# Clustered attention kernel: the spread of the softmax sums and the move of q's low part take other places in the order of issue

## The chip, the cores and the metric

One core of one Trainium2 chip runs the whole kernel in one launch. The metric is device time in microseconds (us), lower is better. Three runs of the kernel before gave 749.48 us as the median (748.42 to 750.17).

## The reference

Attention with a cluster mask feeds two gated mixtures of matrix products. Only the attention is touched by the change:

```python
q_n, k_n, c_n = (x / (norm(x) + 1e-6) for x in (q, k, centroids))
q_assign = argmax(q_n @ c_n.T)          # 16 clusters
k_assign = argmax(k_n @ c_n.T)
scores = where(q_assign == k_assign, q @ k.T / 8, -1e9)
attn = exp(scores - max(scores)); attn = attn / (sum(attn) + 1e-9)
x = attn @ v                            # (2, 8, 768, 64), float32
x = ((x @ w1) * (x @ w2) @ w3) @ w_out  # first mixture
out = (sigmoid(x @ w_gate) * (x @ w_val)) @ w_out2
```

## The kernel before, in words

The kernel has two stages, and the second (the matrix products of the mixtures, from 227 us on) is untouched. The first stage is the attention. It takes the 16 heads as 8 **pairs** `pr` = 0 to 7 of two heads `e` = 0, 1. Each head has 768 queries, taken in three blocks of 256, so that a pair is 6 **blocks**, `at` = 0 to 5. A block is written here as (pair, block): (3, 5) is the sixth block of pair 3. One pass of the loop `for i in range(-2, NB + 2)` writes the instructions of one block for all engines. The order on each engine is the order in which the code is written; nothing reorders it. An instruction that waits therefore holds up all that stands behind it on its engine.

What a block does, by engine:

- **TensorE** (PE): scores of two tiles of 128 queries (`s`, L340), transposes of the exponentials (`pt`, L373), and the products with v (`av`, L415 and L416). Values are carried as a high and a low part, so that a product is made of several.
- **VectorE** (DVE): the row maximum of each score tile (`nm`, L352), the low part of most transposed tiles (`pl`, L403), and pieces of the mask for the next pair. Among these are the comparison with the row's best cluster (`sm`, L268, in `prep_argmax`, block 1) and the one-hot code (`oh`, L279, block 2).
- **ScalarE** (ACT): the exponentials (`e`, L363), the high part of the transposed tiles (`ph`, L391), or a plain copy of them (`pc`, L388) where GpSimd is to split them.
- **GpSimd** (POOL): splits the first transposed tile of blocks 0, 1, 2 and 4 into high (`ph`, L54) and low part (`pl`, L59). It also finishes the pair before: `add_x` (`xa<-xa,xb`, L470, block 3), `norm_x` (`xa<-xa,r`, L474, block 5) and `split_x` (`x`, L54 and L59, right behind).
- **SyncE** (SP) issues every DMA, in the written order. Moves between partitions (`move`, L62) are DMAs too.

How a pair's softmax sums travel: at the end of a pair `turn_sums` and `store_sums` put the reciprocals into DRAM (`r_dram<-rt`, L458). Three blocks into the next pair `spread` (L465) reads them back, each row broadcast to 64 partitions, into the tile `r`. `norm_x` on GpSimd waits for `r`. The tiles `r` and `xb` share one buffer, so `spread` also waits for `add_x`, which reads `xb` last.

How operands are made: for the pair after the next (`later`) the code splits q and k into high and low (`split_lo_q` is the VectorE instruction `lo`, L218). Then `prep_scatter` moves the 64 partitions of a head to their places in the operand tiles `QH`, `KH`, `QX`, `KX`. `prep_mask` moves the one-hot codes of a head behind them (four small moves per head, the tile `ohT`).

Of the kernel before, what the change touches and what calls it, by code (L numbers as in the profile page):

```python
# [27 lines left out]
def tile_cluster_attention__then__moe__then__gated_moe(  # L28
# [32 lines left out]
    def move(dst, src):  # L61
        nc.sync.dma_start(dst.bitcast(F32), src.bitcast(F32))  # L62
# [97 lines left out]
    raw = {}  # L160
# [5 lines left out]
    def load_qk(pr):  # L166
        for w in range(2):
            t = core.tile([128, S], F32, tag="raw", name=f"raw{pr}_{w}", bufs=4)
            nc.sync.dma_start(t, qkT[pr, :, w, :])
            raw[pr, w] = t  # L170

    def load_v(pr, e=None):
        if e != 1:
            raw[pr, "v"] = core.tile([128, 2, KT, D], F32, tag="vraw", name=f"vraw{pr}", bufs=1)
        which = slice(0, 2) if e is None else slice(e, e + 1)
        nc.sync.dma_start(raw[pr, "v"][:, which], v[pr][:, which])


    opnd = {}
# [11 lines left out]
    def split_lo_q(pr):  # L191
        scaled_lo(opnd[pr, "hl"][1], raw[pr, 0], opnd[pr, "hl"][0])
# [20 lines left out]
    def operands(pr, e):  # L213
        opnd[pr, e] = tuple(core.tile([rows, S], F32R, tag=tag, name=f"{tag}{pr}_{e}", bufs=3) for tag, rows in (("QH", 96), ("KH", 96), ("QX", 128), ("KX", 128)))
        return opnd[pr, e]
# [4 lines left out]
    def prep_scatter(pr, e):  # L220
        prep_scatter_hi(pr, e)
        prep_scatter_lo(pr, e)

    def prep_scatter_hi(pr, e):
        qh, ql, kh, kl = opnd[pr, "hl"]
        r = slice(64 * e, 64 * e + 64)
        QH, KH, QX, KX = operands(pr, e)
        parts = [(QH[0:64], qh), (KH[0:64], kh), (QX[0:64], qh), (KX[64:128], kh)]
        if pr > 2:
            parts = parts[1::2] + parts[0::2]  # L230
        for to, part in parts:
            move(to, part[r])

    def prep_scatter_lo(pr, e):
        qh, ql, kh, kl = opnd[pr, "hl"]
        r = slice(64 * e, 64 * e + 64)
        QH, KH, QX, KX = opnd[pr, e]
        move(KX[0:64], kl[r])
        move(QX[64:128], ql[r])

    HALF = S // 2

    def prep_sims(pr):

        sp = ps_t.tile([128, 2, 256], F32, tag="t", name=f"sims{pr}").rearrange("p a b -> p (a b)")
        for n in range(4):
            w, half = divmod(n, 2)
            rows, cols = slice(32 * n, 32 * n + 32), slice(HALF * half, HALF * half + HALF)
            nc.tensor.matmul(sp[rows, 0:HALF], cw[:, pr % NP, :], raw[pr, w][:, cols], start=True, stop=True)
        del raw[pr, 0], raw[pr, 1]  # L250
        opnd[pr, "sims"] = sp

    def prep_sum(pr):
# [32 lines left out]
    def prep_mask(pr, e):  # L286
        ohT = opnd[pr, "oh"]
        QH, KH, _, _ = opnd[pr, e]
        halves = [slice(HALF * h, HALF * h + HALF) for h in range(2)]
        if pr == 0 and e == 0:  # L290
            for h in range(2):
                nc.vector.tensor_scalar(out=KH[64:96, halves[h]], in0=ohT[64 + 32 * h : 96 + 32 * h], scalar1=-1.0, scalar2=BIG, op0=ALU.add, op1=ALU.mult)
                nc.scalar.copy(QH[64:96, halves[h]], ohT[32 * h : 32 * h + 32])
            return
        if pr == 0:
            for h in range(2):
                nc.scalar.activation(KH[64:96, halves[h]], ohT[64 + 32 * h : 96 + 32 * h], AF.Copy, scale=BIG, bias=-BIG)
            nc.scalar.copy(QH[64:96, halves[0]], ohT[0:32])
            move(QH[64:96, halves[1]], ohT[32:64])
            return  # L300
        if e == 0:
            nc.gpsimd.tensor_scalar(out=ohT[64:128], in0=ohT[64:128], scalar1=-1.0, scalar2=BIG, op0=ALU.add, op1=ALU.mult)
        for h in range(2):
            at = 32 * h + C * e
            move(QH[64 : 64 + C, halves[h]], ohT[at : at + C])
            move(KH[64 : 64 + C, halves[h]], ohT[64 + at : 64 + at + C])
# [8 lines left out]
    NB = len(blocks)  # L315
    END = NPR - 1
# [122 lines left out]
    def invert(pr):  # L439

        ss = acc_x[pr, "sum"]
        nc.vector.reciprocal(ss, ss)
# [11 lines left out]
    def store_sums(pr):  # L454
        rp = acc_x.pop((pr, "rp"))
        rt = core.tile([2 * KT, 128], F32, tag="rt", name=f"rt{pr}", bufs=1)
        nc.vector.tensor_copy(rt, rp)
        nc.sync.dma_start(r_dram[pr], rt)  # L458

    def spread(pr, tag, bufs):  # L460

        r = core.tile([128, S], F32, tag=tag, name=f"r{pr}", bufs=bufs)
        for e in range(2):
            row = r_dram[pr, KT * e : KT * e + KT, :].rearrange("t q -> (t q)")
            nc.sync.dma_start(r[64 * e : 64 * e + 64], row.unsqueeze(0).broadcast_to([64, S]))  # L465
        acc_x[pr, "r"] = r

    def add_x(pr):
        xa = acc_x[pr, 0]
        nc.gpsimd.tensor_tensor(out=xa, in0=xa, in1=acc_x[pr, "xb"], op=ALU.add)  # L470
# [63 lines left out]
    hl = [core.tile([128, S], F32R, tag=tag, name=f"{tag}0_{w}", bufs=2) for w in range(2) for tag in ("hi", "lo")]  # L534
    opnd[0, "hl"] = hl
    QH, KH, QX, KX = operands(0, 0)
# [12 lines left out]
    nc.scalar.activation(hl[0][up], q[up], AF.Copy, scale=0.125)  # L549
    prep_split_1_hi(0)  # L550
    prep_sims(0)
    warm(28, "warm2")
    scores(0)
# [29 lines left out]
    if True:  # L583
        for i in range(-2, NB + 2):
            pr, at = divmod(i, 6)
            nxt = pr + 1 if 0 <= i and pr + 1 < NPR else None
            later = nxt + 1 if nxt and nxt + 1 < NPR else None
# [9 lines left out]
            if i == 0:  # L597
                prep_code(0, 1)
                prep_onehot(0, 1)
                prep_turn(0, 1)  # L600
                prep_sims(1)
                prep_sum(1)
            if i == NB - 1:
                store_sums(pr)
            if later and at == 0 and pr:
                load_qk(later)
            if at == 0 and 0 < pr and i < NB:
# [8 lines left out]
            if nxt and nxt > 2 and at == 1:  # L616
                prep_scatter_lo(nxt, 1)
            if nxt and at == 3:
                for e in range(2):
                    if nxt == e == 1:  # L620
                        prep_scatter(1, 1)
                    prep_mask(nxt, e)
                    if nxt == 2 and e == 0:
                        prep_scatter_lo(2, 1)
            split_lo(i - 1, 2)
# [11 lines left out]
                split_x(pr - 1)  # L637
            if nxt == 1 and at == 2:
                load_v(nxt)
            if 0 < pr and i < NB and at == 3:  # L640
                add_x(pr - 1)
                spread(pr - 1, "xb", 1)
            exponentials(2 * i + 3)
# [17 lines left out]
            if i == 1:  # L661
                prep_scatter(1, 0)
            if later and at == 5:
                prep_scatter(later, 0)
            loads = ((6, 2), (7, 1), (7, 3))
            if (pr, at) in loads:
                convert(1 + loads.index((pr, at)))
# [2 lines left out]
            if similar:  # L670
                prep_sims(similar)
# [40 lines left out]
            exponentials(2 * i + 4)  # L712
            if 0 <= i < NB - 2 and at == 4:
                invert(pr)
            if later and pr > 1 and at == 4:
                split_lo_q(later)
            if i == NB - 2:
                end_move(0)
# [37 lines left out]
    at = 0.0  # L756
# [73 lines left out]
    for n, (m, u) in enumerate(order):  # L830
# [6 lines left out]
        if n in W34_AT:  # L837
# [4 lines left out]
            for half in range(2):  # L842
                hl = wo_pool.tile([128, 2, HK, 128], F32R, tag="w3", name=f"w3_{j}_{half}", bufs=3)
# [437 lines left out]
```

## Time and profile before

| what | value |
|---|---|
| three runs, median | 749.48 us (748.42 to 750.17) |
| the profiled execution | 747.86 us |
| its span, first to last instruction | 745.9 us |
| TensorE busy | 738.6 us (99%) |
| VectorE busy | 571.1 us (77%) |
| ScalarE busy | 474.4 us (64%) |
| GpSimd busy | 413.1 us (55%) |
| granted clock of TensorE | 1.0 throughout |

The profile is one execution, taken by the hardware profiler. Busy time is summed over an engine's instructions, "idle before" is the time for which an engine waited ahead of an instruction, and the releaser is what ended that wait. TensorE instructions overlap, so a stall of TensorE shows less as idle time than as a longer distance between two starts.

### The profile page before, as it was taken

The page shows a single profiled execution, that of the slowest core. Times are in us where ns is not written, and L with a number is a line of the kernel's source. Part 1 is how long each engine was busy: PE and PEld are TensorE (multiplying, and loading weights), DVE is VectorE, ACT ScalarE, POOL GpSimd, SP SyncE. Part 2 cuts the span into 40 slices and gives each one's busy share as a digit, 9 for nine tenths or more (in the row PEclk, how much of TensorE's full clock was granted, in tenths as well). Part 3 has the DMA queues.
Part 4 walks back from the last instruction along what each step waited for, and adds up shares of the span by engine and source line. Part 5 has one row for each costly group of instructions (what it writes and reads, how often), then busy time and mean ns, then how long its engine had stood idle before and what let it go on. Part 6 is the DMA issues. An engine that isn't in the chain of part 4 may idle for free.

```text
span 745.9 us, 12286 instructions
## 1 busy us (share of the span) xinstructions
PE 738.6 (99%) x4270; PEld 670.0 (90%) x4270; DVE 571.1 (77%) x894; ACT 474.4 (64%) x994; POOL 413.1 (55%) x420
## 2 busy tenths in 40 slices
PE   8999999999999999999999999999999999999998
PEld 6888999998998888888889999999999999999996
DVE  7999898998986676776743486685686968869675
ACT  8988988988994654645622456767656564565630
POOL 4778878877682655424320046785637555475510
PEclk9999999999999999999999999999999999999999
DMA  6695686677433434434420000221303113030004
GB/s 194 180 219 145 176 225 176 167 173 166 114 110 103 156 114 142 141 113 138 144 85 1 1 29 29 85 85 57 114 10 120 41 58 114 29 113 29 30 0 170
DMA packets 29054, 80.10 MB, mean 107 GB/s; under 512 B 5056, under 2 KB 6656, under 8 KB 28992
## 3 DMA queue, kind: packets, MB, share of 16 engines
q1 hardware_dynamic: 28992, 79.32, 36.1%
q8 instruction: 34, 0.56, 0.3%
q14 instruction: 28, 0.23, 0.1%
HBM read 52.46 MB, written 3.19 MB: 75 GB/s over the span
## 4 chain that ended last, share of the span: by engine, by line
PE 91%; POOL 2%; DVE 2%; ACT 2%; issue 2%; DMA 1%; SPq 0%; POOLq 0%; DVEq 0%; ACTq 0%
PE p L67 13%; PE p L66 13%; PE p L65 13%; PE s L340 7%; PE pt L373 6%; PE p_a L66 4%; PE p_a L67 4%; PE p_a L65 4%; PE av L416 4%; PE av L415 4%; PE p_b L65 2%; PE p_b L66 2%; PE p_b L67 2%; PE w34p L67 2%; PE w34p L66 2%; PE w34p L65 2%
## 5 line engine op out<-in xcount | busy, mean ns | idle before, releaser
L363 ACT ACTIVATE e<-s,nm 128x768 f32<-128x768 f32 x96 | 88.0, 917 | 13.3 <-DVE nm L352 11.0
L352 DVE TENSOR_REDUCE nm<-s 128x1 f32<-128x768 f32 x96 | 90.6, 946 | 7.0 <-PE s L340 6.4
L373 PE MATMUL pt<-ident,e 128*128 128x128 f32 x576 | 86.0, 272 | 0.2 <-DVE sm L256 0.2
L403 DVE TENSOR_TENSOR pl<-pt,ph 128x512 fp32r<-128x512 f32 (+1 forms) x114 | 75.9, 679 | 8.1 <-ACT ph L391 6.8
L415 PE MATMUL av<-ph,vx 128*128 128x256 f32 x288 | 81.0, 308 | 0.4 <-POOL pl L59 0.4
L66 PE MATMUL p<-x,w 128*128 128x512 f32 (+1 forms) x208 | 80.1, 385 | 0.0
L65 PE MATMUL p<-x,w 128*128 128x512 f32 (+1 forms) x208 | 80.1, 385 | 0.0
L67 PE MATMUL p<-x,w 128*128 128x512 f32 (+1 forms) x208 | 80.0, 385 | 0.0
L416 PE MATMUL av<-pl,vx 128*128 128x256 f32 x288 | 74.6, 287 | 0.5 <-DVE pl L403 0.2
L116 POOL TENSOR_TENSOR w_a<-w_f 128x512 uint32<-128x512 uint32 x30 | 32.2, 1072 | 75.9 <-DVE w_f L115 38.1
L373 PEld LDWEIGHTS pt<-ident,e 128*128 128x128 f32 x576 | 67.8, 141 | 4.6 <-DVE sm L256 0.5
L391 ACT CAST ph<-pt 128x512 fp32r<-128x512 f32 x113 | 64.7, 591 | 10.1 <-PE pt L373 9.4
L1160 DVE TENSOR_TENSOR acc<-p,acc 128x512 f32<-128x512 f32 x59 | 40.6, 688 | 29.2 <-PE p L67 28.8
L976 POOL TENSOR_TENSOR wgv_a<-wgv_f 128x512 uint32<-128x512 uint32 x24 | 25.3, 1055 | 66.4 <-DVE wgv_f L975 34.2
L1054 ACT COPY s<-p_a 128x384 f32<-128x384 f32 x72 | 34.6, 481 | 42.9 <-PE p_a L67 42.5
L67 PE MATMUL p<-wo,u 128*128 128x512 f32 (+1 forms) x146 | 57.3, 393 | 0.0
L66 PE MATMUL p<-wo,u 128*128 128x512 f32 (+1 forms) x146 | 57.1, 391 | 0.0
L416 PEld LDWEIGHTS av<-pl,vx 128*128 128x128 f32 x288 | 54.5, 189 | 2.5 <-DVE pl L403 1.1
L65 PE MATMUL p<-wo,u 128*128 128x512 f32 (+1 forms) x146 | 56.3, 386 | 0.0
L340 PE MATMUL s<-KH,QH 80*128 80x512 f32 x192 | 54.5, 366 | 1.4 <-ACT e L363 0.8
L415 PEld LDWEIGHTS av<-ph,vx 128*128 128x128 f32 x288 | 54.3, 189 | 1.5 <-POOL pl L59 0.8
L340 PE MATMUL s<-KX,QX 128*128 128x512 f32 x192 | 49.6, 340 | 0.0
(253 smaller groups left out, 2216.6 us busy)
## 6 DMA issues: line engine op xcount, KB each, us to landing
wgv_f<-in_w_gv_dram SPq DMA_DIRECT2D x24, 512.0 KB, 3.2
wo_f<-in_w_out_dram SPq DMA_DIRECT2D x20, 512.0 KB, 3.2
w_f<-in_w_dram SPq DMA_DIRECT2D x16, 512.0 KB, 3.2
w_f<-in_w3T_dram SPq DMA_DIRECT2D x16, 512.0 KB, 3.1
raw<-in_qkT_dram SPq DMA_DIRECT2D x16, 384.0 KB, 4.5
r<-r_dram SPq DMA_DIRECT2D x16, 192.0 KB, 3.7
xb<-xa SPq DMA_DIRECT2D x15, 192.0 KB, 4.2
out_dram<-acc SPq DMA_DIRECT2D x11, 256.0 KB, 2.0
```

What stands on the lines that cost most here:

```text
L65: nc.tensor.matmul(ps, whi, xhi, start=start, stop=False, skip_group_check=more)
L66: nc.tensor.matmul(ps, whi, xlo, start=False, stop=False, skip_group_check=more)
L67: nc.tensor.matmul(ps, wlo, xhi, start=False, stop=stop, skip_group_check=more)
L340: nc.tensor.matmul(sp[:, c], products[n][0], products[n][1][:, c], start=n == 0, stop=n == 1)
L352: nc.vector.tensor_reduce(out=nms[j], in_=sps[j][:, 0:S], axis=AX.X, op=ALU.max, negate=True)
L363: nc.scalar.activation(et, sps.pop(j)[:, 0:S], AF.Exp, bias=nms.pop(j), accum_out=acc_x[pr, "sum"][:, at : at + 1])
L373: nc.tensor.transpose(pt[:, kk, 128 * t : 128 * t + 128], exps[2 * i + t][:, k0 : k0 + 128], ident)
L391: nc.scalar.copy(ph, pt)
L403: nc.vector.tensor_tensor(out=pl[:, kk], in0=src[:, kk], in1=ph[:, kk], op=ALU.subtract)
L415: nc.tensor.matmul(avs[i], w, ph[:, kk, :], start=kt == 0, stop=False)
L416: nc.tensor.matmul(avs[i], w, pl[:, kk, :], start=False, stop=kt == KT - 1)
L1160: nc.vector.tensor_tensor(out=acc[:, t, :], in0=bk, in1=acc[:, t, :], op=ALU.add)
```

## The change

Three edits, all in the order in which attention writes its instructions; no instruction is added or taken out.

1. In block 3, `add_x` and `spread` of the pair before are written between the masks of the two heads instead of behind both. (The last pair, which prepares no masks, keeps the old place.)
2. `split_lo_q` of `later` is written at the end of block 5 instead of block 4, from pair 2 on.
3. For those pairs the move of q's low part for head 0 (`QX<-lo`) is taken out of the scatter in block 5 and is issued in block 0 of the next pair, behind `store_sums`.

```diff
     def prep_scatter_lo(pr, e):
-        qh, ql, kh, kl = opnd[pr, "hl"]
-        r = slice(64 * e, 64 * e + 64)
-        QH, KH, QX, KX = opnd[pr, e]
-        move(KX[0:64], kl[r])
-        move(QX[64:128], ql[r])
+        prep_scatter_lo_k(pr, e)
+        prep_scatter_lo_q(pr, e)
+
+    def prep_scatter_lo_k(pr, e):
+        move(opnd[pr, e][3][0:64], opnd[pr, "hl"][3][64 * e : 64 * e + 64])
+
+    def prep_scatter_lo_q(pr, e):
+        move(opnd[pr, e][2][64:128], opnd[pr, "hl"][1][64 * e : 64 * e + 64])
...
-        del raw[pr, 0], raw[pr, 1]
...
             if i == NB - 1:
                 store_sums(pr)
+            if nxt and pr > 2 and at == 0:
+                prep_scatter_lo_q(nxt, 0)
...
                     prep_mask(nxt, e)
+                    if e == 0 and pr:
+                        add_x(pr - 1)
+                        spread(pr - 1, "xb", 1)
...
-            if 0 < pr and i < NB and at == 3:
+            if pr == END and i < NB and at == 3:
                 add_x(pr - 1)
                 spread(pr - 1, "xb", 1)
...
             if later and at == 5:
-                prep_scatter(later, 0)
+                prep_scatter_hi(later, 0)
+                prep_scatter_lo_k(later, 0)
+                if pr < 2:
+                    prep_scatter_lo_q(later, 0)
...
-            if later and pr > 1 and at == 4:
+            if later and pr > 1 and at == 5:
                 split_lo_q(later)
```

SyncE in blocks (3, 3) to (4, 0), before (`r_dram<-rt` is the store of the sums, `r<-r_dram` the spread, `ohT` the masks):

```order
L62 DMA KH_0_1580<-ohT_None 16x384
L62 DMA QH_1_1713<-ohT_None 16x384
L62 DMA KH_1_1714<-ohT_None 16x384
L62 DMA QH_1_1713<-ohT_None 16x384
L62 DMA KH_1_1714<-ohT_None 16x384
L465 DMA r_1876<-r_dram 64x768 x2
L62 DMA KH_0_2021<-hi_1_1836 64x768
L62 DMA KX_0_2023<-hi_1_1836 64x768
L62 DMA QH_0_2020<-hi_0_1834 64x768
L62 DMA QX_0_2022<-hi_0_1834 64x768
L62 DMA KX_0_2023<-lo_1_1837 64x768
L62 DMA QX_0_2022<-lo_0_1835 64x768
```

The same place on SyncE now, to the first raw load of (4, 0):

```order
L62 DMA KH_0_1579<-ohT_None 16x384
L467 DMA r_1867<-r_dram 64x768 x2
L62 DMA QH_1_1713<-ohT_None 16x384
L62 DMA KH_1_1714<-ohT_None 16x384
L62 DMA QH_1_1713<-ohT_None 16x384
L62 DMA KH_1_1714<-ohT_None 16x384
...
L62 DMA KX_0_2022<-lo_1_1837 64x768
L460 DMA r_dram<-rt_2061 12x128
L62 DMA QX_0_2021<-lo_0_1835 64x768
L169 DMA raw_0_2084<-in_qkT_dram 128x768
```

The two DMAs of the spread stand ahead of head 1's four mask moves, and `QX<-lo` stands between the store of the sums and the raw loads.

VectorE in blocks (3, 4) to (4, 0), before (`ss` is the reciprocal of the sums, `rt` their copy for the store):

```order
L442 RECIPROCAL ss_1541<-ss_1541 128x12
L218 SCALAR_TENSOR_TENSOR lo_0_1835<-raw_0_1643,hi_0_1834 128x768
L352 TENSOR_REDUCE nm_2000<-s_1987 128x1
L403 TENSOR_TENSOR pl_2_1993<-pt_2_1972,ph_2_1992 128x512
L403 TENSOR_TENSOR pl_0_2004<-pt_0_1995,ph_0_2003 128x512
L256 STREAM_TRANSPOSE sm_2059<-sims_2030 128x384
L352 TENSOR_REDUCE nm_2061<-s_2035 128x1
L457 COPY rt_2063<-s_2035 12x128
L403 TENSOR_TENSOR pl_1_2047<-pt_1_2041,ph_1_2046 128x512
L352 TENSOR_REDUCE nm_2082<-s_2069 128x1
```

The same place on VectorE now:

```order
L444 RECIPROCAL ss_1541<-ss_1541 128x12
L354 TENSOR_REDUCE nm_1999<-s_1986 128x1
L405 TENSOR_TENSOR pl_2_1992<-pt_2_1972,ph_2_1991 128x512
L405 TENSOR_TENSOR pl_0_2003<-pt_0_1994,ph_0_2002 128x512
L258 STREAM_TRANSPOSE sm_2057<-sims_2028 128x384
L354 TENSOR_REDUCE nm_2059<-s_2033 128x1
L459 COPY rt_2061<-s_2033 12x128
L405 TENSOR_TENSOR pl_1_2045<-pt_1_2039,ph_1_2044 128x512
L218 SCALAR_TENSOR_TENSOR lo_0_1835<-raw_0_1643,hi_0_1834 128x768
L354 TENSOR_REDUCE nm_2081<-s_2068 128x1
```

The `lo` instruction has moved behind seven others, from ahead of block 5's first row maximum to ahead of the first row maximum of the next pair's block 0. GpSimd, ScalarE and TensorE keep their orders.

## Rows read from the trace of the kernel before

**Rows 1.** The page: the chain that ended last, share of the span by engine.

```profile
PE 91%; POOL 2%; DVE 2%; ACT 2%; issue 2%; DMA 1%; SPq 0%; POOLq 0%; DVEq 0%; ACTq 0%
```

**Rows 2.** Stretches, blocks 1 to 3, pairs 4 and 5: length, busy by engine.

```profile
126.78:139.22 12.44, 12.44 (x99) 11.91 (x98) 11.75 (x18) 11.48 (x26) 10.18 (x11) 1.00 0.80 207
152.84:165.88 13.04, 13.00 (x99) 12.16 (x98) 12.60 (x18) 11.40 (x27) 9.34 (x10) 1.00 0.85 196
```

**Rows 3.** Stretches, blocks 4 and 5 of pairs 3, 4, 5: the same columns.

```profile
113.23:122.62 9.39, 9.39 (x76) 8.24 (x75) 8.14 (x13) 8.33 (x20) 6.76 (x6) 1.00 0.54 135
139.22:148.70 9.47, 9.47 (x76) 8.20 (x75) 8.16 (x13) 8.48 (x20) 7.86 (x9) 1.00 0.61 154
165.88:175.54 9.66, 9.66 (x76) 8.39 (x75) 8.36 (x13) 8.34 (x20) 7.34 (x8) 1.00 0.58 138
```

**Rows 4.** Waits: engine, line, waited for; us in total, times, longest.

```profile
POOL xa L474 <- DMA r<-r_dram: 13.8, 7, 2.9
```

**Rows 5.** Timeline of GpSimd: start, duration, instruction, idle time before it.

```profile
111.23 1.85 POOL L470 TENSOR_TENSOR xa<-xa,xb 128x768 f32<-128x768 f32 x1
...
117.14 1.29 POOL L59 TENSOR_TENSOR pl<-pc,ph 128x512 fp32r<-128x512 f32 x1
120.89 1.85 POOL L474 TENSOR_TENSOR xa<-xa,r 128x768 f32<-128x768 f32 x1 [2.47 <-DMA r<-r_dram]
...
123.75 1.85 POOL L59 TENSOR_TENSOR x<-xa,x 128x768 fp32r<-128x768 f32 x1
...
129.82 1.71 POOL L59 TENSOR_TENSOR pl<-pc,ph 128x512 fp32r<-128x512 f32 x1
...
155.77 1.28 POOL L59 TENSOR_TENSOR pl<-pc,ph 128x512 fp32r<-128x512 f32 x1
...
205.65 1.29 POOL L59 TENSOR_TENSOR pl<-pc,ph 128x512 fp32r<-128x512 f32 x1
```

**Rows 6.** Timeline of VectorE: pairs 3, 4 and 5.

```profile
118.76 0.90 DVE L218 SCALAR_TENSOR_TENSOR lo<-raw,hi 128x768 fp32r<-128x768 f32 x1
...
123.15 0.67 DVE L403 TENSOR_TENSOR pl<-pt,ph 128x512 fp32r<-128x512 f32 x1
123.74 0.94 DVE L352 TENSOR_REDUCE nm<-s 128x1 f32<-128x768 f32 x1
...
129.82 0.56 DVE L268 TENSOR_TENSOR sm<-sm,mx_None 128x384 f32<-128x384 f32 x1
...
155.88 1.59 DVE L268 TENSOR_TENSOR sm<-sm,mx_None 128x384 f32<-128x384 f32 x1
```

**Rows 7.** Timeline of ScalarE: pairs 4 and 5.

```profile
122.05 0.59 ACT L391 CAST ph<-pt 128x512 fp32r<-128x512 f32 x1 [0.51 <-PE pt L373]
...
125.09 0.92 ACT L363 ACTIVATE e<-s,nm 128x768 f32<-128x768 f32 x1
...
128.30 0.62 ACT L388 COPY pc<-pt 128x512 f32<-128x512 f32 x1
...
154.37 0.62 ACT L388 COPY pc<-pt 128x512 f32<-128x512 f32 x1
```

**Rows 8.** Timeline of SyncE's issues: pair 3 into pair 4.

```profile
113.02 0.59 SPq L62 DMA_DIRECT2D QH<-ohT_None  x1
...
115.60 2.18 SPq L465 DMA_DIRECT2D r<-r_dram  x2
...
123.63 1.28 SPq L169 DMA_DIRECT2D raw<-in_qkT_dram  x2
```

**Rows 9.** The tile r: time from a DMA's issue to its landing.

```profile
DMA to landing us min/median/max: 3.3/3.7/4.1
```

**Rows 10.** Timeline of TensorE: block (7, 1).

```profile
207.00 0.38 PE L416 MATMUL av<-pl,vx 128*128 128x256 f32 x1 [0.18 <-POOL pl L59]
```

**Rows 11.** Stretches, blocks (7, 0) and (7, 1): the columns of rows 2.

```profile
201.14:205.30 4.16, 4.16 (x35) 3.98 (x34) 3.42 (x6) 3.72 (x10) 3.99 (x4) 1.00 0.22 49
205.30:209.90 4.60, 4.41 (x35) 4.04 (x34) 3.30 (x4) 4.22 (x11) 4.29 (x6) 1.00 0.63 185
```

## The prediction

> **What bounds the kernel now.** I read the chain that ended last first: TensorE holds 91% of it, so an edit that frees GpSimd or SyncE pays only where TensorE waited for them [rows 1]. Next come stretches of equal work. Blocks 1 to 3 hold the same 99 TensorE instructions in every pair. They take 12.44 us in pair 4 (2 and 3 read the same), with TensorE busy throughout, and 13.04 us in pair 5 (6 reads the same) [rows 2]. Blocks 4 and 5 take 9.39 us in pair 3 (2 reads the same), 9.47 in pair 4 and 9.66 in pair 5 [rows 3]. So pairs 2 to 4 run at TensorE's own pace and have almost nothing to give. Pairs 5 and 6 lose 0.60 us in blocks 1 to 3, and pair 5 loses 0.27 more behind them.
>
> The third view is the waits: GpSimd waited 13.8 us in seven places for the spread sums `r`, 2.9 at most [rows 4]. That is the wait which the first edit shortens, and none of it is on the chain by itself.
>
> The fourth view, the timelines of GpSimd and VectorE laid side by side, tells why pairs 5 and 6 are slow. VectorE's comparison `sm` (L268) took 0.56 us in pair 4, starting at 129.82, and 1.59 in pair 5, starting at 155.88 [rows 6]. GpSimd's subtraction `pl` (L59) is the mirror: 1.71 us from 129.82 in pair 4, 1.28 from 155.77 in pair 5 [rows 5]. The two do not run together. Whichever starts first runs at its own length and the other is held: in pair 5 VectorE came 0.11 us behind and lost 1.59 - 0.56 = 1.03 us. In pair 4 GpSimd was no earlier than VectorE and lost 1.71 - 1.28 = 0.43 us, which nobody waited for.
>
> The Trainium skill says the same of this pairing (SBUF — State Buffer, "Who interferes with whom"): a VectorE instruction with two inputs in SBUF and a GpSimd instruction that reads SBUF exclude each other for the whole instruction, and the order of issue decides which one is blocked. The trace agrees, with 1.03 us of waiting on one side and 0.43 on the other. By that rule making GpSimd early is a danger to VectorE, which speaks against the first edit; a reading in which both merely share bandwidth would give the no-change rival below.
>
> **The change part by part.**
>
> *Spread between the masks.* The first mask move of head 1 was issued at 113.02, and the spread waited behind four of these until 115.60 [rows 8]. `add_x`, which the spread must follow, ends at 111.23 + 1.85 = 113.08 [rows 5]. So the first of its two DMAs goes at about 113.1 and the second one issue (0.59) later, at 113.7; it lands at most 4.1 us later [rows 8, 9], by 117.8. GpSimd finishes its block-4 split at 117.14 + 1.29 = 118.43 [rows 5]. `norm_x` then starts at about 118.4 instead of 120.89, and its wait of 2.47 us is gone. I take all of it; the bounds are 0 (landing as late as now) and 2.47. Head 1's masks are issued some 1.2 us later and are read some six blocks later, with the next pair's second head; cost nothing, covered by those blocks.
>
> *What is late next.* GpSimd is now ahead, and the next thing that it waits for is ScalarE's copy `pc` of block 1. In pair 5, where GpSimd was early, `pc` ended at 154.37 + 0.62 = 154.99 and `pl` began 0.78 later; VectorE's `sm` came 0.89 after the same end [rows 5 to 7]. In pair 4 `pc` ended at 128.30 + 0.62 = 128.92 and `sm` came 0.90 after it, while `pl` was late by 0.12, at 0.90 [rows 5 to 7]. Take away that lateness and `pl` begins at 128.92 + 0.78 = 129.70, 0.12 ahead of `sm`. So pairs 2, 3 and 4, which have VectorE first today, get pair 5's order: GpSimd first, VectorE held 1.03 us, TensorE late. Each pays 13.04 - 12.44 = 0.60 us in blocks 1 to 3 [rows 2], 1.80 together. Behind them VectorE's delay also holds the mask and with it GpSimd's block-4 split, as in pair 5: 9.66 - 9.39 = 0.27 for pairs 2 and 3, 9.66 - 9.47 = 0.19 for pair 4 [rows 3], 0.73 together. Sum: +2.53 us. Bounds: 0 if VectorE stays first in all three, 2.53 if in none. I take 2.53, since pair 5's relation is the nearest row.
>
> *What it gives.* In block (7, 1) TensorE waits for GpSimd's split of block (7, 0), which ends at 205.65 + 1.29 = 206.94 [rows 5, 10], because `norm_x` of pair 6 had the 2.9 us wait [rows 4]. That block takes 4.60 us, the one before 4.16 [rows 11]. With GpSimd over 2 us earlier this stall of 0.44 us goes; pair 7 has no `sm`, so nothing takes its place. Bounds 0 and -0.44; I take -0.44. Pairs 5 and 6 have GpSimd first already and keep their stall.
>
> *q's low part a block later.* L218 has two inputs in SBUF too, so its place against GpSimd matters. It can start when the `pl` ahead of it is done. That needs `ph`, which ends at 122.05 + 0.59 = 122.64 [rows 7]; with 0.59 (123.15 to 123.74) for `pl` [rows 6] L218 starts at 123.2 to 123.3. GpSimd's `x` split, pulled 2.47 us ahead, ends at 123.75 + 1.85 - 2.47 = 123.13 [rows 5], just in time. L218 (0.90 at most) and the row maximum (0.94) end by 125.1 [rows 6], and ScalarE starts the exponential at 125.09 [rows 7]. Cost: nothing, with hardly a tenth of cover; if the cover goes, the first rival follows. Leaving block 5, L218 frees 0.8 us of VectorE there, where TensorE does not wait in pairs 2 to 4: gain 0, at most the 0.27 of pair 5 [rows 3].
>
> *The move behind the sums' store.* `QX<-lo` now waits for L218 at about 124.1 with the raw loads (123.63 [rows 8]) and the `xb` moves queued behind it, some 1.1 us later than today. It is needed a pair later, the raw loads two blocks later. Cost 0; its other end is the third rival.
>
> **Sum.** +2.53 - 0.44 = +2.1 us. Against its own time the profiled execution goes from 747.86 to 749.9; its span of 745.9 leaves 2.0 us around, unchanged. The median of the runs is 749.48, 1.6 above that execution, so I forecast 749.48 + 2.1 = 751.6 us.
>
> **The rivals.**
>
> *VectorE late enough to win.* Place: the start of pairs 3 to 6. If `r` lands later than about 118.7, GpSimd's `x` split ends behind 123.4, L218 is held, the row maximum misses 125.09, and exponential, `pc` and `pl` slip together. VectorE's `sm`, paced by TensorE, does not. From 0.12 us of slip on `sm` is first. Then pairs 3 to 6 are free: pairs 5 and 6 give back 0.60 + 0.27 + 0.60 = 1.47, pair 7 gives 0.44, pair 2 (no L218 ahead of it) pays 0.87: -1.04, 748.4 us. For it speaks how thin 0.12 us is; against it, that the landing, by 117.8, has 0.9 us to spare.
>
> *No flip.* `r` is early, but the hold does not come about in pairs 2 to 4, because `pl` and `sm` start close and VectorE keeps its place. Only pair 7's 0.44 is left: 749.0 us. For it: in pair 4 VectorE won with the same start to 0.01 us [rows 5, 6]. Against: in pair 5 0.11 us was enough.
>
> *SyncE queue late as well.* `QX<-lo` waits, the raw loads and `xb` moves slip 1.1 us, `add_x` and with it the block-4 split slip in four pairs. If 0.5 us of each reaches TensorE (1.1 less the 0.6 from 117.8 to 118.43 by which the spread has room), +2.0 comes on top: 753.6 us. Against it: the second `xb` move waits for ScalarE's last copy of the pair anyway.
>
> **How the numbers follow.** Forecast 0.58, VectorE late 0.12, no flip 0.22, SyncE queue 0.08. 0.2% is 1.5 us, about what a measurement can tell from no change. The forecast's +2.1 is over it, but with some pairs not flipped (0.87 each) it falls below, a third of its chance. Slower: 0.58 x 0.68 + 0.08 = 0.47, taken as 0.48. Faster needs -1.5, which the first rival reaches only if VectorE stays first in pair 2 as well (-1.9): 0.08 with the other odds. The rest, 0.44, is no change. The range goes from the first rival's 748.4 less half a microsecond of scatter to the forecast with part of the third, 747.9 to 752.8.
>
> **What would show it.** In the profile after, `norm_x` no longer waits for `r` in pairs 2 to 6, and L268 reads about 1.6 us in pairs 2 to 6. Blocks 1 to 3 read 13.04 us in these pairs, and block (7, 1) about 4.16. The forecast is wrong if L268 stays at 0.56 in pairs 3 and 4, or if `norm_x` still waits.

## The result, and the profile after

The change makes the kernel slower. The median of ten runs is 753.65 us (751.27 to 754.64), against 749.30 (747.73 to 751.99) for ten runs of the kernel before: ratio 1.0051, 95% interval 1.0035 to 1.0067, or about 3.8 us (2.6 to 5.0); the two medians are 4.35 us apart. The forecast was 751.6 us with a range up to 752.8, so the sign was right and the size too small. The profiled execution took 751.27 us, with a span of 749.3 where the one before had 745.9: 3.4 us more. It is the fastest of the ten, and one of the four with a mean granted clock of 1.0 (median 752.09 us; 754.07 for the six with 0.998 or 0.999).

All 3.4 us between the two profiled executions lie in the attention. The first matrix product of the mixtures starts at 230.40 us instead of 226.97, 3.43 later, and from there to the end both executions take 518.9 us.

Stretches of the changed kernel: block (1, 5), blocks 1 to 3 of pairs 2 to 6, block (7, 1). The columns are those of [rows 2].

```profile
65.01:72.04 7.04, 5.74 (x44) 4.36 (x43) 5.99 (x10) 4.83 (x11) 5.43 (x5) 1.00 0.71 157
76.20:89.23 13.04, 13.01 (x99) 12.16 (x98) 12.60 (x18) 11.40 (x27) 8.83 (x10) 1.00 0.79 191
103.04:116.08 13.03, 13.02 (x99) 12.18 (x98) 12.60 (x18) 11.40 (x27) 8.80 (x10) 1.00 0.85 226
129.91:142.95 13.04, 13.02 (x99) 12.17 (x98) 12.60 (x18) 11.40 (x27) 8.79 (x10) 1.00 0.83 224
156.75:169.79 13.04, 13.01 (x99) 12.16 (x98) 12.60 (x18) 11.40 (x27) 8.82 (x10) 1.00 0.89 222
183.60:196.63 13.04, 13.01 (x99) 12.17 (x98) 12.60 (x18) 10.85 (x26) 8.79 (x10) 1.00 0.70 198
209.19:213.34 4.15, 4.15 (x35) 3.98 (x34) 3.30 (x4) 4.15 (x11) 3.65 (x6) 1.00 0.62 182
```

All five pairs now read 13.04 us, where only 5 and 6 did [rows 2]. Block (7, 1) went from 4.60 to 4.15 [rows 11]. Blocks 4 and 5 of pairs 2, 3 and 4 answer to [rows 3]:

```profile
89.23:98.89 9.65, 9.62 (x76) 8.31 (x75) 8.19 (x13) 8.25 (x20) 9.32 (x9) 1.00 0.58 140
116.08:125.75 9.68, 9.68 (x76) 8.34 (x75) 8.19 (x13) 8.26 (x20) 9.34 (x9) 1.00 0.54 134
142.95:152.59 9.64, 9.64 (x76) 8.33 (x75) 8.18 (x13) 8.23 (x20) 9.30 (x9) 1.00 0.63 154
```

The comparison and the subtraction of pair 3, on the timelines of VectorE and GpSimd, answer to [rows 5, 6] (line numbers are two higher in the changed kernel, L270 for L268):

```profile
106.08 1.59 DVE L270 TENSOR_TENSOR sm<-sm,mx_None 128x384 f32<-128x384 f32 x1
```

```profile
105.27 0.62 POOL L54 TENSOR_SCALAR ph<-pc 128x512 fp32r<-128x512 f32 x1 [0.60 <-ACT pc L390]
105.97 1.28 POOL L59 TENSOR_TENSOR pl<-pc,ph 128x512 fp32r<-128x512 f32 x1
107.75 1.01 POOL L274 TENSOR_TENSOR sm<-sm,dec 128x384 f32<-128x384 f32 x1 [0.49 <-DVE sm L270]
```

GpSimd is early enough to wait for ScalarE's `pc` (0.60 us), starts its subtraction 0.11 us ahead of the comparison, and the comparison takes 1.59 us instead of 0.56. The wait for `r` is gone: one of 1.4 us is left of 13.8 [rows 4], in the last pair, whose spread was not moved.

```profile
POOL lo L198 <- DMA QX<-lo: 1.4, 1, 1.4
POOL xa L476 <- DMA r<-r_dram: 1.4, 1, 1.4
```

The line of these waits that the prediction did not have is the first. Block (1, 5) took 7.04 us in place of 5.63. This is the block before, with the issue of the two low moves on SyncE:

```profile
65.01:70.64 5.63, 5.48 (x44) 4.30 (x43) 5.58 (x10) 4.73 (x11) 4.71 (x3) 1.00 0.72 189
```

```profile
61.06 0.59 SPq L62 DMA_DIRECT2D KX<-lo  x1
61.69 0.60 SPq L62 DMA_DIRECT2D QX<-lo  x1
```

These are VectorE, TensorE and SyncE of the changed kernel there:

```profile
63.30 0.69 DVE L405 TENSOR_TENSOR pl<-pt,ph 128x512 fp32r<-128x512 f32 x1
66.05 0.96 DVE L218 SCALAR_TENSOR_TENSOR lo<-raw,hi 128x768 fp32r<-128x768 f32 x1 [2.06 <-DMA KX<-lo]
```

```profile
68.53 0.39 PE L418 MATMUL av<-pl,vx 128*128 128x256 f32 x1 [1.14 <-DVE pl L405]
```

```profile
61.16 1.13 SPq L467 DMA_DIRECT2D r<-r_dram  x2
62.33 0.59 SPq L62 DMA_DIRECT2D KX<-lo  x1
62.97 0.59 SPq L62 DMA_DIRECT2D QX<-lo  x1
```

In pair 1, and only there, the two low moves of pair 2's second head stand between the masks of the two heads too. Now the spread is ahead of them and they go 1.3 us later, behind its two DMAs in the queue. They read the buffers into which L218 and GpSimd's L198 are to write the next low parts. So L218 waits 2.06 us, L198 on GpSimd 1.43 (the 1.4 in the list of waits), and TensorE 1.14 for what VectorE has queued behind.

### The profile page after: what moved, and what is told of

Read it like the earlier page. It is cut to its first block, busy times and chain, and to the rows that moved or that the text cites. A ratio compares the mean times of both kernels' runs of the same rounds, so it can differ in the third digit from the quotient of the medians.

```text
span 749.3 us, 12277 instructions
## 1 busy us (share of the span) xinstructions
PE 741.2 (99%) x4270; PEld 671.4 (90%) x4270; DVE 573.6 (77%) x894; ACT 473.9 (63%) x994; POOL 411.8 (55%) x420
## 4 chain that ended last, share of the span: by engine, by line
PE 92%; DVE 2%; ACT 1%; issue 1%; DMA 1%; POOL 1%; SPq 0%; DVEq 0%; POOLq 0%; ACTq 0%
PE p L67 13%; PE p L66 13%; PE p L65 13%; PE s L342 7%; PE pt L375 7%; PE p_a L66 4%; PE p_a L67 4%; PE p_a L65 4%; PE av L418 4%; PE av L417 4%; PE p_b L65 2%; PE p_b L66 2%; PE p_b L67 2%; PE w34p L67 2%; PE w34p L66 2%; PE w34p L65 2%
```

## The experiments

Each kernel ran on the chip beside the kernel before, on the same chip. Spans and block lengths are those of the profiled execution of each.

**The spread alone.** The kernel before, with the first edit only:

```diff
                     prep_mask(nxt, e)
+                    if e == 0 and pr:
+                        add_x(pr - 1)
+                        spread(pr - 1, "xb", 1)
...
-            if 0 < pr and i < NB and at == 3:
+            if pr == END and i < NB and at == 3:
```

> The spread between the masks alone; q's low part and its move stay where they were before. My theory: both losses come from the spread (VectorE's comparison held in pairs 2, 3 and 4, and in pair 1 the low moves of pair 2's second head behind the spread), so this reads as the whole change: profiled span 749.1 to 749.6 us, block (1,5) near 7.0 us, the comparison at 1.59 us in pairs 2 to 6. Rival: the later place of q's low part carries a part of the loss; then the span is at 748.5 or below.

Measured: 757.27 us (ratio 1.0102, 1.0077 to 1.0127), span 754.2. All five comparisons read 1.59 us (1.58 in pair 6), as expected. Block (1, 5) took 7.59 us where near 7.0 was expected: L218 waited 2.61 us there, 0.55 more than in the changed kernel, whose order of instructions is the same up to that place. The span grew by more than twice as much as under the whole change, and neither theory had that. Block (3, 5) takes 7.00 us, 1.77 over the kernel before; (4, 5) takes 7.02. VectorE and GpSimd there:

```profile
123.20 2.50 DVE L218 SCALAR_TENSOR_TENSOR lo<-raw,hi 128x768 fp32r<-128x768 f32 x1
```

```profile
123.03 1.85 POOL L474 TENSOR_TENSOR xa<-xa,r 128x768 f32<-128x768 f32 x1
124.98 1.42 POOL L54 TENSOR_SCALAR x<-xa 128x768 fp32r<-128x768 f32 x1
```

The early `norm_x` starts 0.17 us ahead of L218 in its old place, and L218 takes 2.50 us instead of 0.90 [rows 6]. In (4, 5) the two start 0.15 us apart and L218 takes 2.53. Here the old place of q's low part costs; the second edit takes it out of the way.

**q's low part alone.** The changed kernel with the first edit undone (`spread` again behind both masks, under `0 < pr`):

```diff
                     prep_mask(nxt, e)
-                    if e == 0 and pr:
-                        add_x(pr - 1)
-                        spread(pr - 1, "xb", 1)
...
-            if pr == END and i < NB and at == 3:
+            if 0 < pr and i < NB and at == 3:
```

> q's low part at block 5's end and its move behind the sums' store, without moving the spread. My theory: nothing changes that TensorE waits for: span 745.6 to 746.2 us, the comparison at 0.56 us in pairs 2 to 4. Rival: the later L218 or the raw loads behind its move cost by themselves: 747 or more.

Measured: 752.15 us (ratio 1.0038, 1.0021 to 1.0055), span 750.4. The rival holds. With the spread late, GpSimd's `x` split is still running when L218 comes in its new place, here in block (4, 0) and in the same way in (5, 0):

```profile
124.57 2.36 DVE L218 SCALAR_TENSOR_TENSOR lo<-raw,hi 128x768 fp32r<-128x768 f32 x1
```

```profile
124.27 1.85 POOL L59 TENSOR_TENSOR x<-xa,x 128x768 fp32r<-128x768 f32 x1
126.15 1.26 POOL L54 TENSOR_SCALAR ph<-pc 128x512 fp32r<-128x512 f32 x1
```

Blocks (4, 0) and (5, 0) are 1.19 and 1.22 us longer. Block (3, 5) is 0.85 longer for another reason: in (3, 3) `add_x` waited for the last move of the pair before, which `QX<-lo` in its new place stands ahead of, and TensorE then waited 0.58 us for GpSimd's split:

```profile
112.69 1.84 POOL L472 TENSOR_TENSOR xa<-xa,xb 128x768 f32<-128x768 f32 x1 [0.90 <-DMA xa<-xa]
```

The comparison, expected at 0.56 us in pairs 2 to 4, read 0.81 and 0.87 in pairs 2 and 3 (it began while GpSimd made the high part), 1.61 in pairs 4 and 5, and 0.68 in pair 6. So neither part is free by itself: from the first block of the attention to the first product of the mixtures the first edit alone adds 7.8 us, the others alone 4.1, all three 3.4. The second and third edits were not run apart from each other.

**The low moves first.** The changed kernel with the two low moves of pair 1 issued ahead of the spread again:

```diff
                     prep_mask(nxt, e)
+                    if nxt == 2 and e == 0:
+                        prep_scatter_lo(2, 1)
                     if e == 0 and pr:
                         add_x(pr - 1)
                         spread(pr - 1, "xb", 1)
-                    if nxt == 2 and e == 0:
-                        prep_scatter_lo(2, 1)
```

> The changed kernel with one thing more: in pair 1 the two low moves of pair 2's second head are issued ahead of the spread again. My theory: L218 and GpSimd's k split of block (1,4) no longer wait, block (1,5) is back at 5.6 us and the span is 1.4 us shorter than that of the changed kernel, 747.9 us; the comparison stays held in pairs 2 to 6. Rival: the spread's wait and its two DMAs are late for another reason in pair 1 and the span stays at 749.3.

Measured: 751.53 us (ratio 1.0023, 1.0013 to 1.0032), span 748.0. Block (1, 5):

```profile
65.05:70.68 5.63, 5.47 (x44) 4.30 (x43) 5.59 (x10) 4.73 (x11) 5.54 (x4) 1.00 0.71 162
```

The 1.41 us are gone to the hundredth, all five comparisons still read 1.59, and the kernel stands where the prediction had put the change: 751.53 against 751.6, with 2.1 us of span over the kernel before. The kernel before read 749.67 beside it, so the runs give 1.7 us (1.0 to 2.4).

**GpSimd held back.** The kernel with the low moves first, and in block 1 of pairs 2 to 6 two clears of a small tile between the high and the low part of GpSimd's split:

```diff
-    nc.gpsimd.memset(pad.tile([128, 24], F32, name="pad"), 0.0)
+    hold = pad.tile([128, 24], F32, name="pad")
+    nc.gpsimd.memset(hold, 0.0)
...
         if by_pool(i, k2):
-            split(src, ph, pl, nc.gpsimd, nc.gpsimd)
+            nc.gpsimd.tensor_scalar(out=ph, in0=src, scalar1=1.0, scalar2=1.0, op0=ALU.mult, op1=ALU.mult)
+            if i % 6 == 1 and 1 < i // 6 < END:
+                for _ in range(2):
+                    nc.gpsimd.memset(hold, 0.0)
+            nc.gpsimd.tensor_tensor(out=pl, in0=src, in1=ph, op=ALU.subtract)
```

> As the kernel with the low moves first, and in block 1 of pairs 2 to 6 GpSimd clears a small tile twice between the high and the low part of its split, which starts the subtraction some 0.2 to 0.4 us later. My theory: VectorE's comparison is first in all five pairs and reads 0.56 us, blocks 1 to 3 read 12.44 us everywhere, and the span is 2.5 + 0.87 + 0.60 = about 4.0 us below that of the kernel with the low moves first, near 744.0, under the kernel before. Rival: what slows these pairs is that the sums' DMAs and the early GpSimd work collide with something else; then the span stays within 0.5 us of that kernel.

Measured: 749.30 us (ratio 0.9998, 0.9988 to 1.0008), span 746.5. All five comparisons read 0.56 us and blocks 1 to 3 of pairs 2 to 6 take 12.44 us each, so the order of these two instructions is what makes them slow: adding 0.3 us of work to GpSimd made them 0.60 us shorter. That VectorE was first in all five was partly luck. The two clears put the subtraction only 0.12 us further behind the high part (0.82 us from start to start instead of 0.70), and it began within 0.01 us of the comparison in every pair. The span fell by 1.5 us and not by 4.0, since blocks (3, 5) and (4, 5) are each 1.0 us longer than in the kernel before, and blocks 4 and 5 of pair 5 gave nothing back (9.82 us against 9.66). GpSimd in block (3, 3) and TensorE in (3, 5):

```profile
110.71 0.51 POOL L305 TENSOR_SCALAR ohT_None<-ohT_None 64x384 f32<-64x384 f32 x1 [0.96 <-DMA vraw<-in_v_dram]
112.50 1.87 POOL L477 TENSOR_TENSOR xa<-xa,xb 128x768 f32<-128x768 f32 x1 [1.27 <-DMA xa<-xa]
```

```profile
119.74 0.39 PE L423 MATMUL av<-pl,vx 128*128 128x256 f32 x1 [0.76 <-POOL pl L407]
```

`add_x` waits 1.27 us for the last move of the pair before, and the split behind it reaches TensorE late. In the changed kernel GpSimd came to this place 0.68 us later than in the kernel before (counted from the start of the block), behind the held comparison, and `add_x` shows no wait:

```profile
114.51 1.84 POOL L472 TENSOR_TENSOR xa<-xa,xb 128x768 f32<-128x768 f32 x1
```

That the held comparison hid most of the wait there is argued from these two traces; no run tested it by itself.

**The move behind block 1.** The last kernel, with `QX<-lo` of head 0 issued behind the last moves of block 1:

```diff
-            if nxt and pr > 2 and at == 0:
-                prep_scatter_lo_q(nxt, 0)
...
             if nxt and nxt > 2 and at == 1:
                 prep_scatter_lo(nxt, 1)
+            if nxt and pr > 2 and at == 1:
+                prep_scatter_lo_q(nxt, 0)
```

> The kernel with the low moves first and GpSimd's clears, and the move of q's low part for head 0 issued behind the last moves of block 1 instead of ahead of the raw loads in block 0. My theory: what was left in that kernel (1.03 us in block (3,5), 1.02 in (4,5), 0.1 in (5,4)) came from that move holding up SyncE's queue, so that the last move of the pair before landed 1.3 us late for GpSimd's sum; now that wait is 0.3 us or less, these blocks are back at 5.24 and 5.3 us, and the span is 744.3, 1.5 below the kernel before. Rival: the move only competes for the DMA engines, or the wait comes from the spread: then the blocks stay about 1 us long and the span at 746.4.

Measured: 749.11 us (ratio 0.9995, 0.9982 to 1.0008), span 747.1. Block (3, 5) is back at 5.23 us and (4, 5) at 5.46; `add_x` no longer waits in (3, 3), and 0.45 us in (4, 3). So in this kernel the wait came from the place of that move in SyncE's queue. The span did not follow, for two reasons that were not expected. In block (6, 4), 1.84 us longer, TensorE waits for several DMAs into the operands of pair 7, of which the profile names a mask:

```profile
196.47 0.47 PE L343 MATMUL s<-KH,QH 80*128 80x512 f32 x1 [1.62 <-DMA QH<-ohT_None]
```

```profile
186.82 0.91 SPq L62 DMA_DIRECT2D QX<-lo  x1
187.78 1.24 SPq L89 DMA_DIRECT2D w_f<-in_w_dram  x1
189.79 0.55 SPq L62 DMA_DIRECT2D QH<-ohT_None  x1
```

The mask moves stand behind `QX<-lo` and 512 KB of weights. And in pair 2 the two clears were just too few:

```profile
77.76 1.68 DVE L271 TENSOR_TENSOR sm<-sm,mx_None 128x384 f32<-128x384 f32 x1
```

```profile
77.50 0.29 POOL L406 MEMSET pad<- 128x24 f32 x2
77.75 1.28 POOL L407 TENSOR_TENSOR pl<-pc,ph 128x512 fp32r<-128x512 f32 x1
```

**The hold on the kernel before.** The same two clears, in pairs 5 and 6 of the kernel before and nothing else:

```diff
...
-            split(src, ph, pl, nc.gpsimd, nc.gpsimd)
+            nc.gpsimd.tensor_scalar(out=ph, in0=src, scalar1=1.0, scalar2=1.0, op0=ALU.mult, op1=ALU.mult)
+            if i % 6 == 1 and 4 < i // 6 < END:
+                for _ in range(2):
+                    nc.gpsimd.memset(hold, 0.0)
+            nc.gpsimd.tensor_tensor(out=pl, in0=src, in1=ph, op=ALU.subtract)
```

> The kernel before with one thing more: in block 1 of pairs 5 and 6 GpSimd clears a small tile twice between the high and the low part of its split. My theory: VectorE's comparison is first there and reads 0.56 us instead of 1.59, and the span falls by 0.87 us for pair 5 and 0.60 us for pair 6, from 745.9 to 744.4. Rival: those pairs are slow for another reason (the weights' first loads, say), and the span stays within 0.4 us of 745.9.

Measured: 748.27 us (ratio 0.9984, 0.9973 to 0.9995), span 746.7. Pairs 5 and 6 did as expected: the comparison reads 0.56 and blocks 1 to 3 are 0.6 us shorter in each. The span of the profiled execution rose by 0.8 us all the same. Its attention began 0.55 us later; block (5, 5) became 0.58 longer, where TensorE waited 0.54 us for GpSimd's split after `add_x` had waited 1.05 in (5, 3); and pair 3, whose instructions are those of the kernel before, was held and lost 0.87:

```profile
104.70 1.59 DVE L269 TENSOR_TENSOR sm<-sm,mx_None 128x384 f32<-128x384 f32 x1
```

```profile
103.88 0.62 POOL L401 TENSOR_SCALAR ph<-pc 128x512 fp32r<-128x512 f32 x1 [0.16 <-ACT pc L389]
104.58 1.29 POOL L405 TENSOR_TENSOR pl<-pc,ph 128x512 fp32r<-128x512 f32 x1
```

So which of the two is first in such a pair can change with no change to its instructions: in the kernel before, the comparison of pair 3 was 0.13 us ahead. Over twelve runs this kernel is faster than the one before by 1.2 us (0.4 to 2.0), against 1.5 expected.

**Four clears, and pair 7's move where it was.** The kernel with the move behind block 1, four clears instead of two, and for pair 7 the move in block 0:

```diff
-                for _ in range(2):
+                for _ in range(4):
...
+            if pr == 6 and at == 0:
+                prep_scatter_lo_q(nxt, 0)
...
-            if nxt and pr > 2 and at == 1:
+            if nxt and 2 < pr < 6 and at == 1:
```

> The last kernel (clears, move of q's low part behind block 1's moves) with four clears instead of two, and for pair 7 alone, whose move is issued in pair 6 where no raw loads follow, the move back in block 0. My theory: with two clears GpSimd's subtraction and VectorE's comparison began within 0.01 us of each other and in pair 2 the comparison was held; four clears put GpSimd well behind, so all five comparisons read 0.56 us and pair 2's 0.96 us go; and TensorE's wait of 1.6 us in block (6,4) for a mask move that landed behind the first load of weights goes too. Span 747.1 - 0.96 - 1.8 = 744.3. Rival: the mask move is late because of the weights' load alone; then block (6,4) stays 1.8 us long and the span is 746.2.

Measured: 746.08 us (745.90 to 746.38 in five runs; ratio 0.9954, 0.9942 to 0.9965), span 744.3 as expected. It beats the kernel before by 3.2 us in the medians, and the changed kernel by about 7 (by the ratios 0.9954 and 1.0051, from different series of runs). All five comparisons read 0.56 us, now 0.35 us ahead of the subtraction. Stretches, blocks 1 to 3 of pairs 2 and 5, and block (7, 1):

```profile
74.89:87.34 12.44, 12.44 (x99) 11.91 (x98) 11.88 (x18) 11.52 (x27) 9.63 (x15) 1.00 0.79 209
...
152.87:165.32 12.44, 12.44 (x99) 11.91 (x98) 11.88 (x18) 11.52 (x27) 9.63 (x15) 1.00 0.78 199
...
204.06:208.20 4.14, 4.14 (x35) 3.96 (x34) 3.30 (x4) 4.14 (x11) 3.44 (x6) 1.00 0.63 173
```

**Four clears on the kernel before.** The kernel of the run before last, in pairs 2 to 6 and with four clears:

```diff
-            if i % 6 == 1 and 4 < i // 6 < END:
-                for _ in range(2):
+            if i % 6 == 1 and 1 < i // 6 < END:
+                for _ in range(4):
```

> The kernel before with four clears in block 1 of pairs 2 to 6 and nothing else. My theory: the comparison is first in all five pairs whenever the sums land, blocks 1 to 3 take 12.44 us in each, and the span is 744.4 to 745.2 (some of pair 5's gain is lost where GpSimd's sum now waits for its last move). Rival: GpSimd, late by the clears, holds TensorE instead: then blocks 1 to 3 take 12.6 us or more.

Measured: 747.47 us (ratio 0.9979, 0.9967 to 0.9991), span 744.8. Blocks 1 to 3 of pairs 2 to 6 take 12.44 to 12.46 us. Block (3, 5) is 0.77 us longer than before, with `add_x` waiting 1.01 us in (3, 3) for the last move of the pair before:

```profile
112.13 1.87 POOL L475 TENSOR_TENSOR xa<-xa,xb 128x768 f32<-128x768 f32 x1 [1.01 <-DMA xa<-xa]
```

Here `QX<-lo` is in its old place, so its new place is not the only thing that makes this move late; what did here is open. The rest of what the clears gave is kept. Block (7, 1) reads 4.14 us too, though `norm_x` in (6, 5) still waits 2.69 us for `r`:

```profile
199.06 1.84 POOL L479 TENSOR_TENSOR xa<-xa,r 128x768 f32<-128x768 f32 x1 [2.69 <-DMA r<-r_dram]
```

The clears alone are worth 0.2%. The kernel with four clears and the late move is another 0.25% faster in the runs, but only 0.5 us in the profiled executions, about what block (3, 5) accounts for. It differs by the change's three edits, with the low moves first and `QX<-lo` late, and no run tells what each of these is worth there.

## Why the prediction missed

Point by point, by its steps:

- *The spread lands early and `norm_x` no longer waits*: right. Counted from the start of its pair, `norm_x` in (3, 5) starts 1.5 us earlier and not 2.47, because the held comparison makes the block-4 split ahead of it 1.0 us late.
- *Pairs 2, 3 and 4 get pair 5's order*: right. Blocks 1 to 3 read 13.04 us in each; predicted were 13.04. The blocks behind them read 9.65, 9.68 and 9.64; predicted were 9.66. GpSimd's subtraction began 0.10 to 0.11 us ahead of the comparison, predicted were 0.12. The kernels with GpSimd held back, with two clears and with four, show that this order is the cause.
- *Block (7, 1) gives 0.44 us*: the number is right, 0.45; the cause given is half of it. The wait for `r` alone does not make the stall: with four clears on the kernel before it is still 2.69 us and the stall is gone, as GpSimd's work for pair 6, no longer behind a held comparison, runs 0.6 us earlier, counted from the start of block (7, 1). Either remedy is enough.
- *L218 finds GpSimd just done*: right in all four places, with the first edit in. That the two edits need each other in this way was not in the text; the two runs with one part each showed it.
- *The move behind the sums' store costs nothing*: right for the changed kernel, where `add_x` shows no wait, but by luck: the cover was the held comparison, which the text did not count on. The third rival's mechanism (`add_x` waiting for a late move) is real, 1.27 us once the cover was gone. That its 753.6 us lies next to the measured median is chance, since the changed kernel's trace shows none of that wait.
- *The sum, +2.1 us*: right for the profiled execution but for one term. Without block (1, 5) the attention grew by 3.43 - 1.41 = 2.02 us.

The step that failed is the first part's "cost nothing" for what the spread is moved past; it measured 1.41 us. The prediction counted four mask moves behind it. In pair 1 two more DMAs stand there, the low moves of pair 2's second head, and a VectorE instruction a block later writes into the buffer that they read. The kernel's code has them (`if nxt == 2 and e == 0`) and SyncE's order in pair 1 shows the two rows; the place looked at was pair 3, where they aren't. With these moves first again the kernel measures 751.53 us, against 751.6 forecast.

What stays open is the rest: the profiled executions differ by 3.4 us, the ratio of the runs gives 3.8 (2.6 to 5.0) and the medians 4.35. The forecast with the missed 1.41 us would be 753.0, against 753.65. Two things may make the median run slower than the profiled one, and neither is shown. The wait of L218 in pair 1 is not the same in every execution: it read 2.06 us here and 2.61 in the kernel with the spread alone. The other is the granted clock given with the result.

The scatter from run to run is not explained either. The runs of the other kernels here spread over 2 to 6 us; those with four clears and the late move over 0.5 (five runs). An undecided order of the two instructions would fit that, but four clears on the kernel before, where the comparison was 0.35 us or more ahead in every pair of the profiled execution, still spread over 3.0 (twelve runs).

## What to carry to other kernels

When an engine is freed early, look up what it starts first, and which instruction of another engine that then meets; a wait that nobody else waited for may have been what kept two engines apart. When an issue is moved in a queue, list what it passes in every pass of the loop and not in one, and for each what is to be overwritten behind it. Where two instructions exclude each other and start within a tenth of a microsecond, put the order into the program with a margin.

## What the runs showed of the hardware

Adding idle work to GpSimd made the kernel faster: four clears of a 128x24 tile (0.65 us with their spacing) in five places, on the kernel before, ratio 0.9979. A clear does not hold VectorE's comparison, as the split and the subtraction do. In the kernel with four clears and the late move the comparison in pair 2 began among the clears and took 0.56 us:

```profile
77.93 0.56 DVE L271 TENSOR_TENSOR sm<-sm,mx_None 128x384 f32<-128x384 f32 x1
```

```profile
77.68 0.65 POOL L406 MEMSET pad<- 128x24 f32 x4
```

In the kernel with the low moves first and two clears the comparison in pair 3 started at 103.91 and ran 0.56 us, and the subtraction, begun at the same 103.91, took 1.70:

```profile
103.91 0.56 DVE L271 TENSOR_TENSOR sm<-sm,mx_None 128x384 f32<-128x384 f32 x1
```

```profile
103.65 0.30 POOL L406 MEMSET pad<- 128x24 f32 x2
103.91 1.70 POOL L407 TENSOR_TENSOR pl<-pc,ph 128x512 fp32r<-128x512 f32 x1
```

In pair 2 of the next kernel the two began 0.01 us apart the other way and the comparison took 1.68: a hundredth of a microsecond decides 1 us. A hold passes on. In the kernel with the spread alone `norm_x` ended at 124.88, L218, begun at 123.20, ended 0.82 us after that, at 125.70, and the `x` copy, begun at 124.98, took 1.42 us instead of 0.83.
